# Seven products instead of eight in two more blocks of a retention + bilinear FFN kernel, with the last attention visit divided

## The chip, the cores and the metric

The kernel runs on one core of a Trainium2 chip. The core's engines work side by side, each through its own queue in order: TensorE (PE in the profile; its weight loads are PEld), VectorE (DVE), ScalarE (ACT), GpSimd (POOL), and SyncE (SP), which only issues DMAs. The metric is device time in microseconds (us), lower is better.

## The reference

Retention over a sequence, and then a feed-forward block without an activation function, on 4 x 768 = 3072 tokens of width 512:

```python
def _attn_ref(q, k, v):                      # 4 batches, 8 heads, 768 steps, 64 wide
    gamma = 1.0 - 2.0 ** (-5.0 - np.arange(H))
    for t in range(S):
        state = gamma * state + np.einsum('bhd,bhe->bhde', k[:, :, t], v[:, :, t])
        y[:, :, t] = scale * np.einsum('bhd,bhde->bhe', q[:, :, t], state)
    return y

def _moe_ref(x, w_a, w_b, w_out):            # x: 3072 x 512, d_ff 1536
    a = x @ w_a
    b = x @ w_b
    return (a * b @ w_out)
```

## The kernel before

**Tiles.** The 24 chunks of 128 tokens form eight tiles `J` of 4, 2, 2, 2, 2, 4, 4 and 4 chunks (`TILES`); tile 4 is the fifth. For a tile the kernel computes, for each of 12 blocks `ft` of the hidden width, `a` (`ffn_a`, L598) and `g` (`ffn_g`, L610), each four matmuls of 256 or 512 columns. ScalarE copies `a` out of PSUM as `asb` (L602), VectorE multiplies `g` by it into `ht` (L613). Then `ffn_fast(J, u)`, called the output block here, multiplies `ht` by `w_out` for a pair of chunks.

**Output blocks.** They use seven half-size products instead of eight (a Strassen-like scheme, `product`, L772, six matmuls of 256 columns each). Their left sides are pieces of `ht` and four sums of such pieces, `hsum` (`add`, L670), their banks are R1, R2, R5 and, for the blocks in `ASIDE`, R4. ScalarE keeps a product in `snap` (L784), and VectorE adds two into `osb` (L787, L818). The sum `osb` from R2 and `snap` stands on VectorE behind all `hsum` additions that VectorE makes for the tile. The PSUM pool `ff` has three banks, for `a`, `g`, and R1 to R5.

**Cycles.** In tiles 6 and 7 the `a` of some pairs of blocks `f` is made from seven products too (`seven_a`, called a cycle here): two matmuls of 256 columns for each of parts 1 to 7 (`part_a`, L712), in order 1, 2, 5, then a `g`, then 6, part 4 of the cycle before, 3, another `g`, and 7. R1, R2 and R5 are its banks. ScalarE keeps R1 after part 1, R5 after part 5 and R1 after part 6 (L729, L732, L739), VectorE adds (L726). `SEVEN` gives the pairs: 1 to 3 in tile 6, 1 to 5 in tile 7. `seven_end` finishes the last cycle of a run. The right sides are `xs`, four sums of the tile's input that VectorE makes (`combine_x`, L681), the weights are `ta`, four sums of `w_a` for each pair, made on GpSimd (`combine_a`, L690).

**Visits.** The attention of a pair of chunks runs between these matmuls, in visits (`turn(new, old)`): products of queries with states (`inter`, L359, in two halves), the new pair's states and scores (L287, L317), a tiny copy `mark` (L336) that separates the two halves, the second half, and the products with values (`intra`, L371). Afterwards ScalarE writes the tile's input `xt` from the banks y0 and y1 (`leave`, L386). `begin_turn` and `end_turn` are the two parts of a visit without a new pair. `ahead` lists where each visit stands.

**Order.** `seq` chains every instruction to the one before it on its engine, so each queue follows the order in which the code is written; `later` and `unmasked` hold small jobs that `catch_up` and `mask_now` put in at fixed places. The tile pools add the waits on buffers.

Of the kernel before, what the change touches and what calls it, by code (L numbers as in the profile page):

```python
# [17 lines left out]
ASIDE = ((4, 0), (5, 0), (6, 0), (6, 1), (7, 0))  # L18
SEVEN = {6: (1, 4), 7: (1, 6)}
SPARE = {(J, ft) for J in (2, 3, 4) for ft in range(1, 6 if J == 4 else 10, 2)}  # L20
PAIRS = 3
# [6 lines left out]
def kernel(  # L28
# [349 lines left out]

    def leave(o, c, apart):
# [5 lines left out]
        if apart is None:  # L385
            seq(nc.scalar.copy(dst, src))  # L386
        else:
            on, off = slice(4 - 4 * c, 8 - 4 * c), slice(4 * c, 4 * c + 4)
            part = tra.tile([P, 2, 2, D], F32, tag="kq"[c] + "T2", name="part", bufs=2)
            seq(nc.scalar.copy(part, apart[c][:, :, 2 - 2 * c : 4 - 2 * c]))  # L390
            part = part.rearrange("p s k (par m) -> p s (k par) m", par=2)
            for s in range(2):
                seq(nc.vector.tensor_tensor(dst[:, s, on], src[:, s, on], part[:, s], op=ALU.add))
                seq(nc.vector.tensor_copy(dst[:, s, off], src[:, s, off]))

# [6 lines left out]
    def end_turn(old):  # L402
        inter(old, False, ys[old])
        intra(old)
        later[:] = [lambda c=c: leave(old, c, None) for c in range(2)] + later

    def turn(new, old, eng=nc.scalar):
        catch_up()
        apart = None
        if old is not None:  # L410
            ys[old] = [psat.tile([P, 2, KT, D], F32, tag=f"y{c}", name="y") for c in range(2)]
            if new is None:
                both = psat.tile([P, 2, 2, KT, D], F32, tag="at", name="apart")
                apart = [both[:, c] for c in range(2)]
            inter(old, True, ys[old] if new is not None else apart)
            if new is not None:
                fence[old, 0] = fence[old, 1] = fenced(eng)
        if new is not None:
            chunk_states(new)
            scores(new)  # L420
        if old is not None:
            inter(old, False, ys[old])
            intra(old)
            leaves = [lambda c=c: leave(old, c, apart) for c in range(2)]
            later[:] = leaves + later
# [164 lines left out]
    def ffn_a(J, ft, c0=0, c1=None):  # L590
        c1 = TILES[J] * P if c1 is None else c1
        if J not in ht:
            ht[J] = htp.tile([P, NFT, 4 * P], BF16, tag="ht", name="ht")
        fs = slice(ft * P, (ft + 1) * P)
        a = ff_bank(J, ft, 0, "a")[:, : c1 - c0]
        for kt in range(KT):
            for b0, b1 in parts(J, ft, c0, c1, NFT):
                seq(nc.tensor.matmul(a[:, b0 - c0 : b1 - c0], wa_bf[:, kt, fs], xcols(J, kt, b0, b1),  # L598
                                     start=(kt == 0 and b0 == c0), stop=(kt == KT - 1 and b1 == c1),
                                     skip_group_check=True))  # L600
        asb = asbs[J, ft, c0] = asbp.tile([P, 4 * P], BF16, tag="asb", name="asb")[:, : c1 - c0]
        seq(nc.scalar.copy(asb, a))  # L602

    def ffn_g(J, ft, c0=0, c1=None):
        c1 = TILES[J] * P if c1 is None else c1
        fs = slice(ft * P, (ft + 1) * P)
        g = ff_bank(J, ft, 1, "g")[:, : c1 - c0]
        for kt in range(KT):
            for b0, b1 in parts(J, ft, c0, c1, NFT):
                seq(nc.tensor.matmul(g[:, b0 - c0 : b1 - c0], wb_bf[:, kt, fs], xcols(J, kt, b0, b1),  # L610
                                     start=(kt == 0 and b0 == c0), stop=(kt == KT - 1 and b1 == c1),
                                     skip_group_check=True))
        seq(nc.vector.tensor_tensor(ht[J][:, ft, c0:c1], g, asbs.pop((J, ft, c0)), op=ALU.mult))  # L613
# [77 lines left out]

    banks = {}
# [21 lines left out]

    def seven_a(J, f):

        W2 = 2 * P
        if J not in banks:
            own_banks(J)
        R1, R2, R5 = banks[J][f % 2]  # L720
        snap = raw.tile([P, 4, W2], F32, tag="vf", name="snap")
# [13 lines left out]
        plus(even[:, :W2], R2, snap[:, 0])  # L735
        catch_up(2)
        ffn_g(J, 2 * f - 1)
        part_a(J, f, R1, 6, False)
# [5 lines left out]
        plus(odd[:, :W2], R5, snap[:, 1])  # L744
        catch_up(2)
        ffn_g(J, 2 * f - 2)
        part_a(J, f, R1, 7, False)
# [4 lines left out]

        behind.extend((lambda: plus(odd[:, W2:], R1, snap[:, 2]), last_of))

    behind = []
# [19 lines left out]
    def ffn_fast(J, u):  # L775
# [10 lines left out]
        def plus(dst, R, x):  # L786
            seq(nc.vector.tensor_tensor(dst, R[:, :DH], x, op=ALU.add))  # L787

        R1, R2 = bank(), bank()
# [4 lines left out]
        keep(0, R1)  # L794
        catch_up(2)
        if not swap:
            product(R2, J, u, ("h", 1, 0), (0, 2), True)
        visit(J, "mid")
        plus(osb[:, 0, :DH], R2, snap[:, 0])
# [8 lines left out]
        product(R1, J, u, ("s", 1), (1, 1), False)  # L808
        keep(1, R1)
        catch_up(1)  # L810
        visit(J, "sums", u)
        R5 = bank()
# [8 lines left out]
        else:  # L821
            plus(osb[:, 1, DH:], R1, snap[:, 3])
        if ends:
            seq(nc.sync.dma_start(out=dst[:, 1, DH:], in_=osb[:, 1, DH:]))
# [118 lines left out]
    for j in range(NO):  # L943
# [8 lines left out]
        (4, 0): [(casts, 17)], (4, 8): [(turn, 14, 12)],  # L952
        (4, "o", 0): [(begin_turn, 14), (casts, 18)], (4, "mid"): [(end_turn, 14), (casts, 19)],
        (5, 0): [(casts, 20)], (5, 2): [(casts, 21)], (5, 3): [(turn, 16, None)],
        (5, 8): [(turn, 18, 16), (casts, 22)],
        (5, "sums", 0): [(turn, 20, 18, D_), (casts, 23)],
# [19 lines left out]
    def blocks_seven(J):  # L976
        f0, f1 = SEVEN[J]
        combine_x(J)
        store()
        for ft in range(2 * f0):  # L980
            ffn_a(J, ft)
        for f in range(f0, f1):
            seven_a(J, f)
            sums_of(J, f - 1)
            mask_now(1)
        seven_end(J, f1 - 1)
        sums_of(J, f1 - 1)
        return 2 * f1

    def sums_of(J, f):  # L990
        if J == 6 and f == 0:
            return
        if J == 6:
            f0, f1 = (0, 2) if f == 1 else (f, f + 1)
            for which in range(4):
                add(J, which, f0, f1, nc.gpsimd)
            if f == 3:
                combine_a(4)
                combine_a(5)
        elif f < 5:  # L1000
            for which in range(4 if f < 4 else 2):
                add(J, which, f, f + 1, nc.gpsimd)
        else:
            for which in range(2):
                add(J, which, 5, 6)
            for which in (2, 3):
                add(J, which, 4, 6)

    def blocks(J):
        done = blocks_seven(J) if J in SEVEN else 0  # L1010
        for ft in range(done, NFT):
            if ft > 1 or J == 5:
                store()
            visit(J, ft)
            ffn_ab(J, ft)
            if J in FAST:
                for which, f0, f1 in adds_of(J, ft):
                    if J not in SEVEN or f0 >= 4:
                        add(J, which, f0, f1)

# [48 lines left out]
```

## Time and profile before

| | us |
|---|---|
| runs | 223.07, 222.96, 221.06 (median 222.96) |
| the profiled execution's own time | 222.28 |
| its span | 220.6 |
| TensorE busy | 212.5 (96%) |
| VectorE, ScalarE, GpSimd busy | 147.1, 96.8, 116.5 |

In the profile a row of the timeline gives start, length, engine, line, operation, what is written and read, and in brackets the idle time before it with what ended it. A row's length of matmuls contains a modelled tail, so the pace is read from one start to the next. L numbers are lines of the kernel before.

### The profile page before, as it was taken

What the parts mean: (1) busy time and instruction counts of PE and PEld (TensorE: products, weight loads), DVE (VectorE), ACT (ScalarE), POOL (GpSimd) and SP (SyncE); (2) the same over time, 40 slices, a digit from 0 to 9 for tenths busy, and PEclk for the clock granted to TensorE, in tenths of its full rate; (3) what the DMA queues carried; (4) which work ended last, traced back from release to release, by engine and by line L of the source; (5) the groups of instructions that cost most, each with busy time, mean ns of one, the idle gap of its engine ahead of it and who ended that gap; (6) DMA issues with size and microseconds to landing.
All of it is one profiled execution on the core that took longest, in us unless ns stands there. A gap on an engine that the chain in (4) does not pass through costs nothing.

```text
span 220.6 us, 7028 instructions
## 1 busy us (share of the span) xinstructions
PE 212.5 (96%) x2871; PEld 156.4 (71%) x2875; DVE 147.1 (67%) x325; ACT 96.8 (44%) x239; POOL 116.5 (53%) x157
## 2 busy tenths in 40 slices
PE   8889999999999999999999999989999999999993
PEld 7568888885456887888878445468666478666682
DVE  2774456648816686797785387997877694777731
ACT  3765244342526435436465342736432643443231
POOL 6557799782735435144353514347949960087500
PEclk9999999999999999999999999999999999999999
DMA  5999999997999995896969889799600002200022
GB/s 171 346 377 383 368 314 401 332 203 166 216 257 250 219 248 109 147 234 189 223 126 225 205 147 279 112 230 123 214 0 4 0 3 98 97 0 4 0 95 95
DMA packets 94832, 39.77 MB, mean 180 GB/s; under 512 B 76112, under 2 KB 91728, under 8 KB 94800
## 3 DMA queue, kind: packets, MB, share of 16 engines
q1 hardware_dynamic: 94656, 39.20, 70.2%
q8 instruction: 22, 0.36, 0.6%
q10 hardware_dynamic: 144, 0.13, 0.2%
q14 instruction: 10, 0.08, 0.1%
HBM read 28.31 MB, written 6.29 MB: 157 GB/s over the span
## 4 chain that ended last, share of the span: by engine, by line
PE 85%; DVE 6%; DMA 3%; ACT 2%; issue 1%; POOL 1%; SPq 0%; DVEq 0%; POOLq 0%; ACTq 0%
PE g L610 27%; PE a L598 22%; PE o L772 16%; PE o L647 7%; PE a L712 5%; DMA kf<-in_k_dram 3%; DVE hsum L670 2%; DVE ht L613 2%; POOL kqb L239 1%; PE y L359 1%; PE y L371 1%; PE at L317 1%; PE st L287 1%; ACT xt L386 1%; PE tp L450 1%
## 5 line engine op out<-in xcount | busy, mean ns | idle before, releaser
L613 DVE TENSOR_TENSOR ht<-g,asb 128x256 bf16<-128x256 f32 (+1 forms) x98 | 53.8, 549 | 41.3 <-PE g L610 30.3
L610 PE MATMUL g<-xt,wb_bf 128*128 128x256 bf16 (+1 forms) x432 | 77.8, 308 | 0.3 <-ACT asb L602 0.3
L598 PE MATMUL a<-xt,wa_bf 128*128 128x256 bf16 (+1 forms) x368 | 60.8, 296 | 0.1
L602 ACT CAST asb<-a 128x256 bf16<-128x256 f32 (+1 forms) x82 | 36.9, 452 | 49.5 <-PE a L598 49.2
L610 PEld LDWEIGHTS <-wb_bf 128*128 128x128 bf16 x432 | 42.1, 98 | 16.5 <-issue 0.4
L239 POOL TENSOR_TENSOR kqb<-kf,ktab 128x512 bf16<-128x512 f32 x21 | 22.6, 1081 | 40.7 <-DMA kf<-in_k_dram 31.8
L598 PEld LDWEIGHTS <-wa_bf 128*128 128x128 bf16 x368 | 35.3, 98 | 12.3 <-DVE sums L301 0.3
L239 POOL TENSOR_TENSOR kqb<-qf,qtab 128x512 bf16<-128x512 f32 x21 | 23.1, 1103 | 4.8 <-DMA qf<-in_q_dram 4.6
L204 POOL CAST vb<-vf 128x512 bf16<-128x512 f32 x24 | 14.6, 617 | 18.8 <-DMA vf<-in_v_dram 9.3
L772 PEld LDWEIGHTS <-hsum 128*128 128x128 bf16 x216 | 20.9, 98 | 3.7 <-DVE sums L301 0.6
L784 ACT COPY snap<-o 128x256 f32<-128x256 f32 x32 | 12.0, 376 | 21.2 <-PE o L772 21.1
L670 POOL TENSOR_TENSOR hsum<-ht 128x256 bf16<-128x256 bf16 (+1 forms) x15 | 11.0, 735 | 18.5 <-DVE ht L613 18.5
L772 PE MATMUL o<-wt_bf,hsum 128*128 128x256 bf16 x162 | 19.8, 273 | 0.4 <-DVE sums L301 0.3
L772 PEld LDWEIGHTS <-ht 128*128 128x128 bf16 x162 | 15.4, 98 | 2.8
L647 PE MATMUL o<-wo_bf,ht 128*128 128x512 bf16 x69 | 15.9, 379 | 0.2
L670 DVE TENSOR_TENSOR hsum<-ht 128x256 bf16<-128x256 bf16 (+1 forms) x32 | 13.5, 426 | 0.3
L301 DVE TENSOR_TENSOR sums<-st,sums 128x256 f32<-128x256 f32 x30 | 12.7, 423 | 1.5
L772 PE MATMUL o<-wo_bf,ht 128*128 128x256 bf16 x108 | 13.3, 273 | 0.0
L202 ACT CAST gst<-sums 128x256 bf16<-128x256 f32 x33 | 12.7, 417 | 0.5 <-DVE sums L299 0.3
L787 DVE TENSOR_TENSOR osb<-o,snap 128x256 f32<-128x256 f32 x22 | 9.2, 419 | 5.2 <-PE o L772 3.3
L647 PEld LDWEIGHTS <-ht 128*128 128x128 bf16 x72 | 6.9, 98 | 7.9
L323 DVE TENSOR_TENSOR aT<-at,mask 128x512 bf16<-128x512 f32 x18 | 12.1, 680 | 0.0
(99 smaller groups left out, 260.9 us busy)
## 6 DMA issues: line engine op xcount, KB each, us to landing
out_dram<-osb SPq DMA_DIRECT2D x11, 512.0 KB, 4.4
kf<-in_k_dram SPq DMA_DIRECT2D x18, 256.0 KB, 4.2
qf<-in_q_dram SPq DMA_DIRECT2D x36, 128.0 KB, 3.9
vf<-in_v_dram SPq DMA_DIRECT2D x18, 256.0 KB, 4.2
wsta<-in_moe_w_a_dram SPq DMA_DIRECT2D x6, 512.0 KB, 7.7
wstb<-in_moe_w_b_dram SPq DMA_DIRECT2D x6, 512.0 KB, 7.9
wsto<-in_moe_w_out_dram SPq DMA_DIRECT2D x6, 512.0 KB, 7.5
kf<-in_k_dram SPq DMA_DIRECT2D x3, 512.0 KB, 5.9
```

The source lines that it names most:

```text
L202: seq(nc.scalar.copy(dst, src))
L204: seq(engine.tensor_copy(dst, src))
L239: seq(eng.tensor_tensor(dst, src, tab, op=ALU.mult))
L301: seq(nc.vector.tensor_tensor(new, u[c][:, s], old, op=ALU.add))
L323: unmasked.append(lambda r=r: seq(nc.vector.tensor_tensor(aT[n][:, r].rearrange("p s h d -> p (s h) d"), at[:, r].rearrange("p s h d -> p ...
L598: seq(nc.tensor.matmul(a[:, b0 - c0 : b1 - c0], wa_bf[:, kt, fs], xcols(J, kt, b0, b1), start=(kt == 0 and b0 == c0), stop=(kt == KT - 1 a ...
L602: seq(nc.scalar.copy(asb, a))
L610: seq(nc.tensor.matmul(g[:, b0 - c0 : b1 - c0], wb_bf[:, kt, fs], xcols(J, kt, b0, b1), start=(kt == 0 and b0 == c0), stop=(kt == KT - 1 a ...
L613: seq(nc.vector.tensor_tensor(ht[J][:, ft, c0:c1], g, asbs.pop((J, ft, c0)), op=ALU.mult))
L647: seq(nc.tensor.matmul(o, ht[J][:, ft, i * P : (i + 1) * P], wo_bf[:, f, 2 * r : 2 * r + 2, :].rearrange("p a d -> p (a d)"), start=(ft == ...
L670: seq(eng.tensor_tensor(s[which], x(), y(), op=op))
L772: seq(nc.tensor.matmul(R[:, :DH], lhs, (wo_bf, wt_bf)[w][:, f, m, :], start=(first and f == 0), stop=(f == NH - 1), skip_group_check=True))
```

## The change

- `SEVEN` lists the pairs themselves: 1, 2, 4, 5 for tile 6 and 0 to 5 for tile 7, four and six cycles instead of three and five. Pairs 0 and 3 of tile 6 are made in the plain way.
- The first cycle of tile 7 is spread over the second output block of tile 6 (`begin_seven`, `step_seven`), and `combine_x(7)` stands before that block.
- The banks of a cycle are taken for each cycle (`own_banks(J, f)`). R5 is always the first half of the tile `at`. In pair 4 of tile 6 the banks are y0, the state bank and a bank of `ff`; in pair 5, R1 is the second half of the tile whose first half is R5.
- In tile 6, the visit with the last new pair comes earlier (before block 6 instead of 8), its masks are put in at once, and the last visit (pair 22) is divided: `begin_turn` inside pair 5's cycle, `end_turn` before the first output block. The path with the separate bank `apart` is gone.
- In tile 4, `begin_turn` and `end_turn` of pair 14 come later within the first output block, and the `catch_up(2)` in block 8 is gone.
- `mark` of the visit in tile 5's first output block moves from VectorE to ScalarE.
- GpSimd makes the sums `hsum` of tiles 6 and 7 for pairs 0 to 3 two pairs at a time, and all four sums of pair 4; VectorE makes those of pair 5 alone. `combine_a` runs for pairs 1, 2, 4, 5 in tile 5, and 0 and 3 at the end of tile 6.
- The first output block of tile 6 computes R2 before R1 (`swap`), as that of tile 7 did.
- `ht` is taken in `ffn_g` instead of `ffn_a`; `SPARE` is written another way and holds the same.

```diff
-SEVEN = {6: (1, 4), 7: (1, 6)}
+SEVEN = {6: (1, 2, 4, 5), 7: (0, 1, 2, 3, 4, 5)}
@@ turn: "apart" removed; leave() only copies
-            if new is None:
-                both = psat.tile([P, 2, 2, KT, D], F32, tag="at", name="apart")
@@ ffn_ab
-        if (J, ft) == (4, 8):
-            catch_up(2)
@@ the banks of a cycle
-    def own_banks(J):
-        at = psat.tile([P, 2, 4 * P], F32, tag="at", name="a")
-        st = psst.tile([P, 4 * P], F32, tag="st", name="a")
-        y = [psat.tile([P, 4 * P], F32, tag=f"y{c}", name="a") for c in range(2)]
-        banks[J] = [[y[f % 2][:, : 2 * P], st[:, : 2 * P], at[:, f % 2, : 2 * P]] for f in range(2)]
+    def own_banks(J, f):
+        st = psst.tile([P, 4 * P], F32, tag="st", name="a")
+        if (J, f) == (6, 4):
+            y = psat.tile([P, 4 * P], F32, tag="y0", name="a")
+            at = psff.tile([P, 4 * P], F32, tag="ff", name="a")
+        else:
+            both = psat.tile([P, 2, 4 * P], F32, tag="at", name="a")
+            at = both[:, 0]
+            if (J, f) == (6, 5):
+                y = both[:, 1]
+            else:
+                y = psat.tile([P, 4 * P], F32, tag=f"y{f % 2}", name="a")
+        return [x[:, : 2 * P] for x in (y, st, at)]
@@ ffn_fast
-        swap = (J, u) == (7, 0)
+        swap = u == 0 and J in SEVEN
@@ ahead (a line or two)
-        (6, 8): [(turn, 22, 20)], (6, "o", 0): [(turn, None, 22)],
+        (6, 6): [(turn, 22, 20), (catch_up, 2), (mask_now,)], (6, 11): [(begin_turn, 22)], (6, "o", 0): [(end_turn, 22)],
+        (6, "before", 1): [(combine_x, 7), (begin_seven, 7, 0)],
+        (6, 1, 1): [(step_seven,)], (6, 3, 1): [(step_seven,)], (6, 5, 1): [(step_seven,)],
-    ahead[5, "sums", 0] += [(combine_a, f) for f in (1, 2, 3)]
+    ahead[5, 4, 0] += [(combine_a, f) for f in (1, 2, 4, 5)]
@@ sums_of
+        if f < 4:
+            if f % 2:
+                for which in range(4):
+                    add(J, which, f - 1, f + 1, nc.gpsimd)
+        else:
+            for which in range(4):
+                add(J, which, f, f + 1, nc.gpsimd if f == 4 else nc.vector)
+            if (J, f) == (6, 4):
+                combine_a(0)
+                combine_a(3)
```

**Where instructions move.** First, TensorE at the start of a cycle. Before, in tile 6, pair 2 (names with their buffer numbers, and in brackets the engine whose signal a row waits for): parts 1, 2 and 5 write three tiles.

```order
L712 MATMUL a_3594<-xt_3238,wa_bf_172 128x256
L712 LDWEIGHTS wa_bf_172
L712 MATMUL a_3593<-xt_3238,wa_bf_172 128x256 [waits DVE_49]
L712 LDWEIGHTS wa_bf_172
L712 MATMUL a_3593<-xt_3238,wa_bf_172 128x256
L712 LDWEIGHTS ta_3470 [waits Pool_49]
L712 MATMUL a_3592<-xs_3571,ta_3470 128x256 [waits DVE_49]
```

Now, in tile 6, pair 5, the cycle that holds `begin_turn(22)`:

```order
L703 MATMUL a_3888<-xt_3238,wa_bf_172 128x256
L703 LDWEIGHTS wa_bf_172
L703 MATMUL a_3887<-xt_3238,wa_bf_172 128x256 [waits DVE_49]
L703 LDWEIGHTS wa_bf_172
L703 MATMUL a_3887<-xt_3238,wa_bf_172 128x256
L703 LDWEIGHTS ta_3470 [waits Pool_49]
L703 MATMUL a_3888<-xs_3575,ta_3470 128x256 [waits Activation_49]
```

Parts 1 and 5 now write the same tile `a_3888`, and part 5 waits for ScalarE, which keeps part 1's result, instead of VectorE.

Second, TensorE in the first output block of tile 6, where R5 begins (the tile `o` with `hsum_3664` before, and `hsum_3670` now). Before:

```order
L772 LDWEIGHTS hsum_3665 [waits DVE_49]
L772 MATMUL o_4009<-wt_bf_175,hsum_3665 128x256
L772 LDWEIGHTS hsum_3665 [waits DVE_49]
L772 MATMUL o_4009<-wt_bf_175,hsum_3665 128x256
L772 LDWEIGHTS hsum_3664
L772 MATMUL o_4052<-wt_bf_175,hsum_3664 128x256 [waits Activation_49]
```

Now:

```order
L779 LDWEIGHTS hsum_3671 [waits Pool_49]
L779 MATMUL o_4026<-wt_bf_175,hsum_3671 128x256
L779 LDWEIGHTS hsum_3671 [waits DVE_49]
L779 MATMUL o_4026<-wt_bf_175,hsum_3671 128x256
L779 LDWEIGHTS hsum_3670
L779 MATMUL o_4059<-wt_bf_175,hsum_3670 128x256 [waits DVE_49]
```

R5 waited for ScalarE's copy out of R4's bank; now it has R2's bank and waits for VectorE's `osb`. In the first output blocks of tiles 5 and 7 it waits for VectorE in both kernels.

Third, VectorE in the first output block of tile 5. Before:

```order
L670 TENSOR_TENSOR hsum<-ht,hsum 128x256 x2
L787 TENSOR_TENSOR osb<-o,snap 128x256
L336 COPY mark<-bq 128x1
L301 TENSOR_TENSOR sums<-st,sums 128x256 x4
L818 TENSOR_TENSOR osb<-o,snap 128x512
L323 TENSOR_TENSOR aT<-at,mask 128x512
```

Now:

```order
L655 TENSOR_TENSOR hsum<-ht,hsum 128x256 x2
L794 TENSOR_TENSOR osb<-o,snap 128x256
L301 TENSOR_TENSOR sums<-st,sums 128x256 x4
L828 TENSOR_TENSOR osb<-o,snap 128x512
L323 TENSOR_TENSOR aT<-at,mask 128x512
```

`mark` is gone from this queue; it stands on ScalarE behind the copy of R1.

More of the change, by code (lines that the diff above doesn't have):

```diff
@@ L384, in leave @@
         src = ys[o][c].rearrange("p s k (par m) -> p s (k par) m", par=2)
[L385 to L394, printed above, removed]
+        seq(nc.scalar.copy(dst, src))
     def begin_turn(old, eng=nc.scalar):
@@ L753, in seven_a, with begin_seven, step_seven @@
         behind.extend((lambda: plus(odd[:, W2:], R1, snap[:, 2]), last_of))
+        yield
+    def seven_a(J, f):
+        steps = seven_steps(J, f)
+        next(steps)
+        catch_up(2)
+        ffn_g(J, 2 * f - 1)
+        next(steps)
+        catch_up(2)
+        ffn_g(J, 2 * f - 2)
+        visit(J, 2 * f + 1)
+        next(steps)
+    amid = []
+    def begin_seven(J, f):
+        amid.append(seven_steps(J, f))
+    def step_seven():
+        next(amid[0])
     behind = []
```

92 lines of the change are left out of this document (39 added, 53 removed).

## The prediction

> **What bounds the kernel now.** I read the page first, then TensorE's timeline from tile 4 to the end, then the other queues at each place where TensorE stood or may stand.
>
> ```profile
> span 220.6 us, 7028 instructions
> PE 212.5 (96%) x2871; PEld 156.4 (71%) x2875; DVE 147.1 (67%) x325; ACT 96.8 (44%) x239; POOL 116.5 (53%) x157
> PEclk9999999999999999999999999999999999999999
> ```
>
> TensorE is busy for 96% of the span at full granted clock. So fewer matmul columns shorten the time directly, and every wait of TensorE that the change takes away or brings in counts in full. The profiled execution took 222.28 us, 1.68 more than its span, and lies 0.68 below the median of the three runs. I sum against 222.28.
>
> **Two more cycles.** Two cycles of tile 7 show the pace:
>
> ```profile
> 128.84 1.03 PE L598 MATMUL a<-xt,wa_bf 128*128 128x512 bf16 x4
> 129.70 1.03 PE L610 MATMUL g<-xt,wb_bf 128*128 128x512 bf16 x4
> ...
> 192.32 0.60 PE L712 MATMUL a<-xt,wa_bf 128*128 128x256 bf16 x4
> ...
> 195.57 0.60 PE L712 MATMUL a<-xt,wa_bf 128*128 128x256 bf16 x4
> ```
>
> A plain group of four takes 129.70 - 128.84 = 0.86. A cycle takes 195.57 - 192.32 = 3.25, of which two g groups are 1.73; its 14 half-width matmuls take 1.52 (0.11 each) and replace two plain a groups of 1.73. Saved: 0.21 per cycle, **-0.43** for two.
>
> **Tile 4.** After the visit the leaves and state casts that `catch_up(2)` puts in delay ScalarE's `asb`, whose bank the next g needs:
>
> ```profile
> 113.35 0.60 PE L598 MATMUL a<-xt,wa_bf 128*128 128x256 bf16 x4
> 114.22 0.60 PE L610 MATMUL g<-xt,wb_bf 128*128 128x256 bf16 x4 [0.27 <-ACT asb L602]
> 114.68 0.60 PE L598 MATMUL a<-xt,wa_bf 128*128 128x256 bf16 x4
> 115.11 0.60 PE L610 MATMUL g<-xt,wb_bf 128*128 128x256 bf16 x4
> ```
>
> The step from a to g is 0.87 where the next is 0.43: 0.44 lost, and with one leaf per block instead of two it goes. But `end_turn(14)` now stands after the fourth product, so both its leaves come after ScalarE's last `snap` of the block, and tile 5 needs them:
>
> ```profile
> 119.36 0.37 ACT L784 COPY snap<-o 128x256 f32<-128x256 f32 x1 [0.28 <-PE o L772]
> 119.63 0.59 ACT L386 CAST xt<-y 128x512 bf16<-128x512 f32 x1
> 120.11 0.39 ACT L784 COPY snap<-o 128x256 f32<-128x256 f32 x1
> ...
> 138.78 1.08 ACT L386 CAST xt<-y 128x512 bf16<-128x512 f32 x2
> ```
> ```profile
> 121.20 1.03 PE L598 MATMUL a<-xt,wa_bf 128*128 128x512 bf16 x4
> ```
>
> A `snap` holds its queue 0.27 (119.36 to 119.63), two leaves 1.08: 120.11 + 0.27 + 1.08 = 121.46, after the 121.20 at which tile 5 began. So 0.25 comes back (between 0 and 0.44): **-0.19**.
>
> **The mark in tile 5.**
>
> ```profile
> 148.78 0.28 PE L359 MATMUL y<-kqT,gst 64*64 64x64 bf16 x10 [0.95 <-DVE mark L336]
> ...
> 149.28 1.48 PE L772 MATMUL o<-wt_bf,hsum 128*128 128x256 bf16 x12
> ```
> ```profile
> 148.25 0.41 DVE L787 TENSOR_TENSOR osb<-o,snap 128x256 f32<-128x256 f32 x1
> 148.59 0.14 DVE L336 COPY mark<-bq 128x1 f32<-128x1 f32 x1
> ```
>
> `mark` sits on VectorE behind hsum additions and the `osb` from R2; TensorE idles 0.95. On ScalarE it follows the copy of R1, which nothing delays, so that wait goes, and the late `osb` is next: the product that starts at 149.28 is R5's, in R2's bank, which that `osb` frees at 148.66. With 0.05 for the signal, R5 starts at 148.71: **-0.57**, not -0.95. Nothing waits behind `mark` on ScalarE for long, whose next job is R5's own copy.
>
> **The divided last visit.**
>
> ```profile
> 115.64 0.32 PE L359 MATMUL y<-kqT,gst 64*64 64x64 bf16 x16
> 115.89 1.48 PE L772 MATMUL o<-wo_bf,ht 128*128 128x256 bf16 x12
> ...
> 117.84 0.83 PE L772 MATMUL o<-wt_bf,ht 128*128 128x256 bf16 x6
> ...
> 176.75 1.03 PE L610 MATMUL g<-xt,wb_bf 128*128 128x512 bf16 x4
> ...
> 178.34 1.48 PE L772 MATMUL o<-wo_bf,ht 128*128 128x256 bf16 x12
> ```
>
> Whole, it takes from the end of a g (176.75 + 0.86) to 178.34: 0.73. Divided as in tile 4, the first part takes 115.89 - 115.55 = 0.34 (115.11 plus 0.44), the second 117.84 - 117.20 = 0.64 (twelve products after 115.89): **+0.25**. The `apart` additions that go were on VectorE and ended none of TensorE's waits; the masks put in at once stand on VectorE before it is needed.
>
> **Pair 5's cycle in tile 6.** R1 and R5 are now halves of one tile, and the program makes part 5 wait for ScalarE's copy of part 1, and by the same tile part 3 for the copy of part 6. In separate tiles neither wait exists, so the trace has no row for it; its length follows from a cycle of tile 7:
>
> ```profile
> 192.74 0.37 ACT L729 COPY snap<-a 128x256 f32<-128x256 f32 x1 [1.15 <-PE a L712]
> ```
>
> The copy starts 0.42 after its part (192.32) and ends at 0.79; with 0.05 the waiting matmul starts at 0.84, where it would have started after two parts, at 0.44. Twice 0.40: **+0.80** (between 0, if the halves didn't wait, and 0.80). The GpSimd sums do not depend on it.
>
> **R5 in the first output blocks.** R5 must wait for the `osb` from R2, which stands behind VectorE's hsum additions, and those are slowed when GpSimd works:
>
> ```profile
> 178.77 0.75 DVE L670 TENSOR_TENSOR hsum<-ht 128x256 bf16<-128x256 bf16 x1
> 179.55 0.64 DVE L670 TENSOR_TENSOR hsum<-hsum,ht 128x256 bf16<-128x256 bf16 x1
> 207.82 0.69 DVE L613 TENSOR_TENSOR ht<-g,asb 128x512 bf16<-128x512 f32 x1 [0.61 <-PE g L610]
> 208.61 0.29 DVE L670 TENSOR_TENSOR hsum<-ht 128x256 bf16<-128x256 bf16 x1
> ...
> 209.82 0.42 DVE L787 TENSOR_TENSOR osb<-o,snap 128x256 f32<-128x256 f32 x1
> ```
> ```profile
> 164.77 1.15 POOL L670 TENSOR_TENSOR hsum<-ht 128x512 bf16<-128x512 bf16 x1 [3.04 <-DVE ht L613]
> ...
> 169.34 0.67 POOL L670 TENSOR_TENSOR hsum<-ht 128x256 bf16<-128x256 bf16 x1
> ...
> 171.97 0.67 POOL L670 TENSOR_TENSOR hsum<-ht 128x256 bf16<-128x256 bf16 x1
> ...
> 178.65 0.72 POOL L690 TENSOR_TENSOR ta<-wa_bf 128x256 bf16<-128x256 bf16 x1
> ...
> 202.91 0.67 POOL L670 TENSOR_TENSOR hsum<-ht 128x256 bf16<-128x256 bf16 x1 [0.58 <-DVE ht L613]
> ...
> 206.91 0.67 POOL L670 TENSOR_TENSOR hsum<-hsum,ht 128x256 bf16<-128x256 bf16 x1
> ```
> ```profile
> 209.54 2.23 PE L772 MATMUL o<-wt_bf,hsum 128*128 128x256 bf16 x18
> ```
>
> An addition of 0.29 alone takes 0.64 to 0.75 beside GpSimd: the one at 178.77 ends at 179.52, 0.15 after the GpSimd instruction that ran when it began (179.37); one addition per GpSimd instruction. In tile 7 GpSimd was done at 207.58, a second before VectorE's additions. Now, from 202.91, it makes four double sums (169.34 - 164.77 = 4.57) and four single ones (171.97 - 169.34 = 2.63), until 210.1. VectorE's four additions, from 208.61, then end behind GpSimd's at about 208.9, 209.6 and 210.2, the fourth at 210.5; the `osb` after them ends at 210.95 instead of 210.24. R1's product ends at 209.54 + 6 x 0.11 = 210.2, R5 started 0.1 later behind that `osb`, and now would at 211.0: **+0.70** (0 to 0.8).
>
> In tile 6 R5 took R4's bank and waited for nothing on VectorE; now it takes R2's. GpSimd has the same eight sums and then eight `combine_a` instructions, so it is busy throughout. From the last `ht` to `osb`'s end are 0.1 + four additions (2.0 to 2.6) + 0.4; TensorE needs `end_turn` (0.64) and, as from 208.51 to 210.2 in tile 7, 1.7 until R5. The wait is 0.2 to 0.8 (0 if the additions ran free): **+0.60**.
>
> One rule of the Trainium skill bears on this, in "SBUF — State Buffer", section "Who interferes with whom": a VectorE instruction with both inputs in SBUF and a GpSimd instruction that reads SBUF exclude each other, and the later one is held until the other has finished. The 0.75 and 0.64 agree, except that a held addition ends 0.15 after GpSimd's, not its full 0.29. By the rule word for word each R5 would be about 0.14 later, and the sum 0.3 higher.
>
> Covered: the sums themselves (GpSimd's second sum of pair 4 is due about 208.9, its matmul about 210.0), and `ta` for pairs 4 and 5, made seconds ahead. TensorE issues the interleaved first cycle of tile 7 at the usual pace if `xs` is there (a rival, below).
>
> **Sum.** -0.43 - 0.19 - 0.57 + 0.25 + 0.80 + 0.70 + 0.60 = **+1.16**: 223.4 from the profiled execution, 224.1 from the median. I take 223.7. A difference under 1% (2.2 us) is about what this kernel's runs cannot tell from none, so the forecast is "same", on its slow side.
>
> **Rivals.** *The new waits are covered*: R1 and R5 don't wait on each other's copies, or the additions slip between GpSimd's instructions. For it: VectorE has fewer additions than before in tile 6. Against it: the 0.64 to 0.75 above. Time: -0.43 - 0.19 - 0.57 + 0.25 = -0.94, 221.3; if `osb` also came early enough for all 0.95, 220.9.
>
> *`combine_x(7)` blocks the second output block of tile 6.* It stands on VectorE before the `osb` that frees R5's bank there, and GpSimd may still be in `combine_a`:
>
> ```profile
> 155.73 0.41 DVE L681 TENSOR_TENSOR xs<-xt 128x512 bf16<-128x512 bf16 x1
> ...
> 157.68 0.89 DVE L681 TENSOR_TENSOR xs<-xt 128x512 bf16<-128x512 bf16 x1
> ```
>
> Beside GpSimd four of these took 157.68 + 0.89 - 155.73 = 2.84. With 0.5 before them and 0.8 behind, R5's bank is free 4.1 after the block began; TensorE wants it after five products and ten matmuls of the cycle, 34 x 0.11 = 3.7. That is 0.4, and the parts waiting for each `xs` can lose as much again; with the word-for-word additions (0.3) the sum is about 2.3: 224.6, slower. It decides if GpSimd ends `combine_a` later than about 1 us into the block; by its own rows it ends about when the block begins.
>
> *The cycles save nothing* (half-width matmuls slower): the cycle of 3.25 speaks against it; 223.8.
>
> **Chances.** Forecast 0.62, covered 0.18 (a third of it below -1%), blocked 0.14, no saving 0.03, else 0.03. Faster by over 1%: 0.08; within: 0.75; slower: 0.17. Range: the covered case at its usual 221.3 to the blocked one with the median's 0.68, 225.2.
>
> **What would show it.** The cycle steps of 3.25 unchanged; no 0.95 behind `mark`, but R5 in tile 5 starting right behind `osb`; part 5 in pair 5's cycle idle 0.4 behind ScalarE; R5 in tiles 6 and 7 idle behind VectorE's `osb`, with additions of 0.6 and more. Wrong, if those last three idle times are absent.

## The result, and the profile after

The changed kernel takes 223.41 us (median of 11 runs, 222.47 to 224.18), the kernel before 222.07 in the same session (11 runs): a ratio of 1.0064, with a 95% interval of 1.0043 to 1.0085. That is 1.34 us more, inside the 1% called "same", on its slow side; the interval excludes 1, so the loss itself is clear of noise. The profiled execution took 223.99 us, 1.71 more than that of before.

The page of the changed kernel (its first lines, and the chain):

```profile
span 222.3 us, 7055 instructions
PE 212.3 (96%) x2887; PEld 157.2 (71%) x2887; DVE 150.2 (68%) x318; ACT 97.6 (44%) x245; POOL 120.4 (54%) x155
...
PE 80%; DVE 10%; DMA 3%; ACT 3%; issue 2%; POOL 1%; SPq 0%; DVEq 0%; ACTq 0%
```

TensorE's busy time hardly moved (212.5 before). VectorE's share of the chain (the work that ended last, followed back) went from 6% to 10%. The waits of TensorE name where (us in total, how many, the longest):

```profile
PE o L779 <- DVE osb L794: 2.0, 4, 0.9
...
PE y L359 <- DVE ht L600: 0.3, 1, 0.3
PE st L287 <- DVE ht L600: 0.3, 1, 0.3
PE a L703 <- ACT snap L718: 0.2, 1, 0.2
PE a L703 <- ACT snap L727: 0.2, 1, 0.2
```

The longest, `osb`, is four waits: 0.27 in tile 3, ahead of the places that the change moves, 0.49 in tile 5 in place of the 0.95 behind `mark`, and 0.32 and 0.90 in tiles 6 and 7. These last two and the two of `snap` are the waits that the change brought in. The next table is made from TensorE's timeline of both kernels: each row is the time from the first matmul of one place to the first matmul of the next (the end of a g of tile 4 is its start plus 0.44).

| stretch (us) | before | after | difference |
|---|---|---|---|
| start to the end of the g of tile 4's block 7 | 110.01 | 109.70 | -0.31 |
| the visit in tile 4's block 8, until its a | 1.58 | 2.32 | +0.74 |
| blocks 8 to 11 of tile 4, to the last g | 3.52 | 3.07 | -0.45 |
| tile 4's last g and output block, to tile 5 | 6.09 | 6.42 | +0.33 |
| tile 5's blocks | 22.94 | 22.83 | -0.11 |
| tile 5's output blocks | 11.79 | 11.22 | -0.57 |
| tile 6's blocks with the last two visits | 22.41 | 23.24 | +0.83 |
| first output block of tile 6 | 4.63 | 5.08 | +0.45 |
| second output block of tile 6, to the cycle of pair 2 in tile 7 | 9.35 | 9.19 | -0.16 |
| the other cycles of tile 7 | 15.23 | 15.23 | 0 |
| first output block of tile 7 | 4.70 | 5.66 | +0.96 |
| the rest | 8.35 | 8.34 | -0.01 |

The sum is 1.70, the difference of the spans. The +0.83 of tile 6's blocks is made up of one more cycle (-0.21), pair 5's two waits (+0.82, below) and the divided visit (+0.22, further below). Now the rows of after for the three places that lose. Pair 5's cycle in tile 6 (TensorE's timeline: start, length, line, what is written and read, idle time before):

```profile
171.84 0.60 PE L703 MATMUL a<-xt,wa_bf 128*128 128x256 bf16 x4
172.69 0.38 PE L703 MATMUL a<-xs,ta 128*128 128x256 bf16 x2 [0.24 <-ACT snap L718]
...
173.98 0.38 PE L703 MATMUL a<-xt,ta 128*128 128x256 bf16 x2
174.61 0.38 PE L703 MATMUL a<-xs,wa_bf 128*128 128x256 bf16 x2 [0.24 <-ACT snap L727]
```

Part 5 comes 0.85 after part 1 instead of 0.44, part 3 comes 0.63 after part 4 instead of 0.22: 0.41 each, 0.82 together. The brackets say only 0.24, because a matmul's recorded length holds a modelled tail; the steps from start to start tell the loss.

The first output block of tile 7, first TensorE, then VectorE, then GpSimd:

```profile
210.29 0.81 PE L779 MATMUL o<-wt_bf,hsum 128*128 128x256 bf16 x6
212.00 1.47 PE L779 MATMUL o<-wt_bf,hsum 128*128 128x256 bf16 x12 [0.90 <-DVE osb L794]
```
```profile
209.29 0.29 DVE L655 TENSOR_TENSOR hsum<-ht 128x256 bf16<-128x256 bf16 x1
209.62 0.64 DVE L655 TENSOR_TENSOR hsum<-hsum,ht 128x256 bf16<-128x256 bf16 x1
210.18 0.76 DVE L655 TENSOR_TENSOR hsum<-ht 128x256 bf16<-128x256 bf16 x1
210.86 0.75 DVE L655 TENSOR_TENSOR hsum<-ht,hsum 128x256 bf16<-128x256 bf16 x1
211.54 0.41 DVE L794 TENSOR_TENSOR osb<-o,snap 128x256 f32<-128x256 f32 x1
```
```profile
204.01 1.15 POOL L655 TENSOR_TENSOR hsum<-ht 128x512 bf16<-128x512 bf16 x1 [2.25 <-DVE ht L600]
...
209.32 0.79 POOL L655 TENSOR_TENSOR hsum<-hsum,ht 128x256 bf16<-128x256 bf16 x1
210.07 0.72 POOL L655 TENSOR_TENSOR hsum<-ht 128x256 bf16<-128x256 bf16 x1
210.75 0.72 POOL L655 TENSOR_TENSOR hsum<-ht,hsum 128x256 bf16<-128x256 bf16 x1
```

VectorE's last three additions end at 210.26, 210.94 and 211.61, each 0.14 or 0.15 after one of GpSimd's (210.11, 210.79, 211.47). `osb` ends at 211.95 and R5 starts at 212.00. TensorE was ready at 210.29 + 0.65 = 210.94 (six matmuls of 0.11), so R5 waited 1.06; before it waited 0.1. In tile 6 it is the same with 0.48 (product at 180.78, R5 at 181.91):

```profile
180.78 0.82 PE L779 MATMUL o<-wt_bf,hsum 128*128 128x256 bf16 x6
181.91 1.47 PE L779 MATMUL o<-wt_bf,hsum 128*128 128x256 bf16 x12 [0.32 <-DVE osb L794]
```

### The profile page after: what moved, and what is told of

It reads as the page before. It is cut to its first block, busy times and chain, and to the rows that moved or that the text cites. A ratio compares the mean times of both kernels' runs of the same rounds, so it can differ in the third digit from the quotient of the medians.

```text
span 222.3 us, 7055 instructions
## 1 busy us (share of the span) xinstructions
PE 212.3 (96%) x2887; PEld 157.2 (71%) x2887; DVE 150.2 (68%) x318; ACT 97.6 (44%) x245; POOL 120.4 (54%) x155
## 4 chain that ended last, share of the span: by engine, by line
PE 80%; DVE 10%; DMA 3%; ACT 3%; issue 2%; POOL 1%; SPq 0%; DVEq 0%; ACTq 0%
PE g L595 27%; PE a L583 20%; PE o L779 12%; PE o L632 7%; PE a L703 7%; DVE hsum L655 4%; DVE ht L600 3%; DMA kf<-in_k_dram 3%; PE y L359 1%; PE at L317 1%; ACT xt L385 1%; PE st L287 1%; PE tp L437 1%; DVE osb L794 1%; PE y L371 1%
## 5 line engine op out<-in xcount | busy, mean ns | idle before, releaser
L583 PE MATMUL a<-xt,wa_bf 128*128 128x256 bf16 (+1 forms) x352 | 56.7, 292 | 0.2
L587 ACT CAST asb<-a 128x256 bf16<-128x256 f32 (+1 forms) x78 | 34.5, 443 | 44.1 <-PE a L583 43.2
L583 PEld LDWEIGHTS <-wa_bf 128*128 128x128 bf16 x352 | 33.8, 98 | 10.8 <-issue 0.3
L239 POOL TENSOR_TENSOR kqb<-qf,qtab 128x512 bf16<-128x512 f32 x21 | 22.6, 1079 | 6.7 <-DMA qf<-in_q_dram 6.5
L779 PE MATMUL o<-wt_bf,hsum 128*128 128x256 bf16 x162 | 20.4, 272 | 1.8 <-DVE osb L794 1.7
L655 POOL TENSOR_TENSOR hsum<-ht 128x512 bf16<-128x512 bf16 (+1 forms) x12 | 11.9, 995 | 17.1 <-ACT snap L718 11.7
L715 DVE TENSOR_TENSOR asb<-a,snap 128x256 bf16<-128x256 f32 x30 | 12.0, 418 | 2.2 <-ACT snap L727 0.8
L655 DVE TENSOR_TENSOR hsum<-ht 128x256 bf16<-128x256 bf16 (+1 forms) x30 | 12.4, 416 | 0.3
```

What stands on the lines that cost most here:

```text
L239: seq(eng.tensor_tensor(dst, src, tab, op=ALU.mult))
L655: seq(eng.tensor_tensor(s[which], x(), y(), op=op))
L779: seq(nc.tensor.matmul(R[:, :DH], lhs, (wo_bf, wt_bf)[w][:, f, m, :], start=(first and f == 0), stop=(f == NH - 1), skip_group_check=True))
```

## The experiments

Ratios are to the kernel before, whose runs lay between the others on the same chip. Its median there was 221.62 for the first four kernels, 221.41 for the next four, 221.60 for the last three.

### R1 and R5 in separate tiles

```diff
-        if (J, f) == (6, 4):
+        if (J, f) == (6, 5):
+            y = psat.tile([P, 2, 4 * P], F32, tag="at", name="a")[:, 0]
+            at = psff.tile([P, 4 * P], F32, tag="ff", name="a")
+        elif (J, f) == (6, 4):
...
-            if (J, f) == (6, 5):
-                y = both[:, 1]
-            else:
-                y = psat.tile([P, 4 * P], F32, tag=f"y{f % 2}", name="a")
+            y = psat.tile([P, 4 * P], F32, tag=f"y{f % 2}", name="a")
```

> The changed kernel, but in pair 5's cycle of tile 6 R1 and R5 are separate tiles (R5 a bank of ff, as in pair 4). Theory (the shared tile makes parts 5 and 3 wait for ScalarE's copies): part 5 starts 0.44 us after its cycle instead of 0.85, part 3 starts 0.22 after part 4 instead of 0.63, and the kernel is 0.8 us shorter than the changed one, about 222.6. Rival (the two idle times are signals or the divided visit that stands in that cycle): the steps of 0.85 and 0.63 stay, no gain. The wait for R5 in the first output block of tile 6 should stay or grow, since GpSimd's sums don't move.

Measured: 222.60 us, ratio 1.0056 (1.0034 to 1.0079, four runs). Pair 5's cycle in TensorE's timeline:

```profile
171.56 0.60 PE L703 MATMUL a<-xt,wa_bf 128*128 128x256 bf16 x4
172.00 0.38 PE L703 MATMUL a<-xs,ta 128*128 128x256 bf16 x2
...
173.30 0.38 PE L703 MATMUL a<-xt,ta 128*128 128x256 bf16 x2
173.52 0.38 PE L703 MATMUL a<-xs,wa_bf 128*128 128x256 bf16 x2
```

The steps are 0.44 and 0.22, both waits are gone, and tile 6's blocks take 22.44 instead of 23.24: 0.80. The shared tile was the cause. R5's wait in the output block stayed, at 0.52. The whole kernel's ratio fell by 0.0008, less than 0.80 would give (0.0036); with four runs that isn't settled by the times.

### Two additions behind osb

```diff
         plus(osb[:, 0, :DH], R2, snap[:, 0])
+        if swap:
+            for which in (2, 3):
+                add(J, which, 5, 6)
...
-            for which in range(4):
+            for which in range(4 if f == 4 else 2):
                 add(J, which, f, f + 1, nc.gpsimd if f == 4 else nc.vector)
```

> The changed kernel, but in the first output blocks of tiles 6 and 7 VectorE makes the last two of pair 5's four hsum additions behind the osb from R2. Theory (R5 waits because osb stands behind four slowed additions): R5's idle time of 0.32 to 0.48 us in tile 6 and of 0.90 to 1.06 in tile 7 both go, so 1.4 us shorter than the changed kernel, about 222.0. The additions themselves stay slow (0.6 to 0.8 each). Rival (osb is late for another reason, ScalarE's copy or the bank): the idle times stay, or the third product waits for the moved additions and the gain is lost, 223.4.

Measured: 222.21 us, ratio 1.0029 (1.0006 to 1.0051). In tile 7 the first output block takes 4.61 instead of 5.66, so R5's wait is gone with 1.05 gained, although two additions there still take 0.64 and 0.75. In tile 6 the block takes 4.78 instead of 5.08: R5's wait went, but the next product of R1 then stood 0.18, behind ScalarE's second copy of R1, which stood behind two leaves. And most of the rest was lost in the next block, where VectorE makes the sums `xs` (the first of them on VectorE, then TensorE):

```profile
183.72 0.77 DVE L666 TENSOR_TENSOR xs<-xt 128x512 bf16<-128x512 bf16 x1
```
```profile
183.83 0.60 PE L703 MATMUL a<-xt,wa_bf 128*128 128x256 bf16 x4
184.55 0.38 PE L703 MATMUL a<-xs,ta 128*128 128x256 bf16 x2
```

Part 5 starts 0.72 after part 1 instead of 0.44, since the first `xs` takes 0.77 beside GpSimd's `combine_a`. From the start of tile 6's first output block to the cycle of pair 1 in tile 7 it is 10.96 against 11.02: of 0.48, 0.06 is left. A wait that goes uncovered the next two.

### GpSimd's sums of tile 7 one pair at a time

```diff
-        if f < 4:
+        if f < 4 and J == 7:
+            for which in range(4):
+                add(J, which, f, f + 1, nc.gpsimd)
+        elif f < 4:
             if f % 2:
```

> The changed kernel, but in tile 7 GpSimd makes the sums of pairs 0 to 3 one pair at a time, so that it ends its work earlier, at about 209.5 instead of 211.5 us, close to where VectorE's four additions begin. Order on VectorE and banks unchanged. Theory (GpSimd's sums slow the additions): the four additions in tile 7 take about 0.3 each instead of 0.64 to 0.76, R5's idle time there falls from 0.90 to 0.1 or less, about 0.9 us shorter than the changed kernel, 222.5. Rival (the additions are slow by themselves, or osb waits for something else): they keep 0.64 to 0.76 and the idle time of 0.9 stays. Tile 6 is unchanged and keeps its wait.

Measured: 222.17 us, ratio 1.0037 (1.0010 to 1.0065). VectorE's additions and GpSimd's last sum in tile 7:

```profile
207.87 0.44 DVE L655 TENSOR_TENSOR hsum<-ht 128x256 bf16<-128x256 bf16 x1
208.34 0.29 DVE L655 TENSOR_TENSOR hsum<-hsum,ht 128x256 bf16<-128x256 bf16 x1
208.55 0.28 DVE L655 TENSOR_TENSOR hsum<-ht 128x256 bf16<-128x256 bf16 x1
208.75 0.28 DVE L655 TENSOR_TENSOR hsum<-ht,hsum 128x256 bf16<-128x256 bf16 x1
```
```profile
207.49 0.67 POOL L655 TENSOR_TENSOR hsum<-ht,hsum 128x256 bf16<-128x256 bf16 x1
```

GpSimd ends at 208.16. The two traces differ in their start of the output block (206.87 here, 208.30 in the changed kernel), so times are compared from there: GpSimd ends 1.29 after it, where the changed kernel had 3.17 and the expectation 1.2. The one addition that meets it ends at 208.31, 0.15 later; the other three take 0.28 or 0.29, with the order of VectorE's work and the banks as in the changed kernel. R5 doesn't wait, and the block takes 4.60 instead of 5.66. So it was GpSimd's sums that made VectorE late.

### Mark alone

```diff
-        (5, "sums", 0): [(turn, 20, 18, D_), (casts, 23)],
+        (5, "sums", 0): [(turn, 20, 18), (casts, 23)],
```

> The kernel before with one edit: mark of the visit in tile 5's first output block is on ScalarE instead of VectorE. Theory: the wait of 0.95 us behind mark goes, and R5 becomes the next to wait, for VectorE's osb, so only 0.5 to 0.6 are gained: 221.5 against 222.07. Rival (nothing else is late there): 0.95 gained, 221.1. Second rival (the queue of ScalarE is as late): no gain.

Measured: 221.18 us, ratio 0.9984 (0.9961 to 1.0008). In the trace tile 5's output blocks take 10.86 instead of 11.79, as if all 0.95 were gained, and the wait for `osb` is short (0.22). The times allow anything from a loss of 0.18 to a gain of 0.86. The theory fits the times and not the trace, the first rival the trace and, by a little, not the times; the last two runs below take up this stretch again.

### Tile 4's visit put back, and the catch_up alone

In the changed kernel:

```diff
-        (4, "o", 0): [(casts, 18)], (4, "mid", 0): [(begin_turn, 14)], (4, 4, 0): [(end_turn, 14), (casts, 19)],
+        (4, "o", 0): [(begin_turn, 14), (casts, 18)], (4, "mid", 0): [(end_turn, 14), (casts, 19)],
```

> The changed kernel, but in tile 4's output block the two parts of the visit of pair 14 stand where they stood before (first part ahead of the block, second after the second product); the catch_up(2) stays away. Theory (the late leaves cost tile 5's start): from the last g of tile 4 to tile 5's first matmul 6.10 us as before the change, instead of 6.42, so 0.3 shorter than the changed kernel, 223.1. Rival (tile 5 started late for another reason): 6.4 stays.

In the kernel before:

```diff
-        if (J, ft) == (4, 8):
-            catch_up(2)
```

> The kernel before with one edit: the catch_up(2) in tile 4's block 8 is gone. Theory (the two leaves and casts delayed asb): the step from a to g of block 10, 0.87, becomes 0.44, 0.44 gained, about 221.6 against 222.07, and the visit's second part doesn't lose it again. Rival (the leaves are only moved to the next blocks, where they delay another asb): another step of 0.6 to 0.9 appears, no gain.

Measured: 223.62 us, ratio 1.0114 (1.0078 to 1.0151, four runs), for the first, and 221.15, ratio 0.9998 (0.9979 to 1.0017), for the second. My expectation failed in both. Blocks 8 to 11 take 3.07 in both, as hoped, but from the last g to tile 5 it is 6.78 in both, where the kernel before has 6.09 and the changed one 6.42. The rows are of the kernel with the visit put back, TensorE and then ScalarE:

```profile
114.88 0.26 PE L359 MATMUL y<-kqT,gst 64*64 64x64 bf16 x8
115.64 0.26 PE L359 MATMUL y<-kqT,gst 64*64 64x64 bf16 x8 [0.50 <-ACT gst L202]
```
```profile
114.87 1.02 ACT L202 CAST gst<-sums 128x256 bf16<-128x256 f32 x3
```

The `catch_up(2)` also put in the casts of the states, `gst`. Without it three of them are still to do when `begin_turn` starts, and TensorE waits 0.50 for them (0.51 in the other of the two kernels). The later visit gives ScalarE time for these casts; what the late leaves cost (0.33) is less than what the early visit would (0.69). The two edits of tile 4 are one.

### One cycle less

```diff
-SEVEN = {6: (1, 2, 4, 5), 7: (0, 1, 2, 3, 4, 5)}
+SEVEN = {6: (1, 2, 4, 5), 7: (1, 2, 3, 4, 5)}
...
-        (6, "before", 1): [(combine_x, 7), (begin_seven, 7, 0)],
-        (6, 1, 1): [(step_seven,)], (6, 3, 1): [(step_seven,)], (6, 5, 1): [(step_seven,)],
...
-        if J == 6:
-            combine_x(J)
+        combine_x(J)
...
-                combine_a(0)
```

> The changed kernel with one cycle less: pair 0 of tile 7 is made in the plain way, with the input sums at the head of tile 7 as before. Theory (a cycle of seven products replaces 1.73 us of matmuls by 1.52): from the start of tile 6's second output block to tile 7's third cycle 0.16 to 0.21 longer than in the changed kernel, about 223.6. Rival (the interleaved cycle costs what it saves, because VectorE makes the input sums beside GpSimd): equal or shorter, down to 223.2.

Measured: 223.14 us, ratio 1.0075 (1.0045 to 1.0106). From the second output block of tile 6 to the cycle of pair 2 it takes 9.34, against 9.19 in the changed kernel: the cycle saves 0.15, of 0.21; 0.06 is lost at its part 5. The times can't tell 0.15 from nothing.

### The new waits taken out together

The edits of the first two experiments, and these:

```diff
-        catch_up(2)
+        catch_up(1 if (J, u) == (6, 0) else 2)
...
-        catch_up(1)
+        if (J, u) != (6, 0):
+            catch_up(1)
...
-        if swap:
+        if swap or (J, u) == (5, 0):
             for which in (2, 3):
-                add(J, which, 5, 6)
+                add(J, which, 4 if J == 5 else 5, 6)
...
-        (4, "o", 0): [(casts, 18)], (4, "mid", 0): [(begin_turn, 14)], (4, 4, 0): [(end_turn, 14), (casts, 19)],
+        (4, "o", 0): [(begin_turn, 14), (casts, 18)], (4, "mid", 0): [(end_turn, 14), (casts, 19)],
...
+        if (J, ft) == (5, 11):
+            return [(1, 4, 5), (0, 5, 6), (1, 5, 6)]
```

> The changed kernel with its new waits taken out together: separate tiles for R1 and R5 in pair 5's cycle of tile 6; in the first output blocks of tiles 5, 6 and 7 the last two hsum additions behind the osb from R2; tile 4's visit where it stood before; one leaf instead of two ahead of R1's second copy in tile 6. Theory (each wait stands by itself): 0.80 + 0.48 + 0.96 + 0.32 + 0.3 = 2.9 us shorter than the changed kernel, 220.5, a ratio to the kernel before of about 0.993. Rival (as one wait goes, another queue is late at the same place): half of that, 222.0, a ratio of 1.0.

Measured: 221.38 us, ratio 1.0008 (0.9987 to 1.0030): the rival's side. Tile 6's blocks (22.43) and tile 7's first output block (4.61) gain in full. Tile 4 loses 0.36, as in the two runs above, and tile 6's first output block gains 0.40, of which the second block and its cycle give back 0.33 (6.27 instead of 5.94), by `xs` additions of 0.77 to 0.88. This trace also has 23.42 for tile 5's blocks, 0.59 more than the changed kernel's; the second version below, with the same code there, has 22.82, so that is no effect of the edits.

So a second version has tile 4 as in the changed kernel, and `combine_a(0)` moved into GpSimd's idle time after the first double sums of tile 6:

```diff
                 for which in range(4):
                     add(J, which, f - 1, f + 1, nc.gpsimd)
+                if (J, f) == (6, 1):
+                    combine_a(0)
...
             if (J, f) == (6, 4):
-                combine_a(0)
                 combine_a(3)
```

> The changed kernel with R1 and R5 in separate tiles, the last two hsum additions behind the osb from R2 in tiles 5 to 7, one leaf ahead of R1's second copy in tile 6, tile 4 as in the changed kernel, and GpSimd's combine_a for pair 0 moved into its idle time after the first double sums of tile 6, so that it is done before VectorE makes the sums of tile 7's input. Theory (what the run with the tile 4 visit put back lost was 0.36 in tile 4, and 0.33 in tile 6's second block to additions slowed by combine_a): 0.7 shorter than that run, 220.7 on the same chip, a ratio to the kernel before of 0.995 to 0.997, and the second block of tile 6 with its cycle takes 5.9 us again. Rival (the sums of the input wait for the leaves or for osb, not for GpSimd): the block keeps 6.2, and the ratio is 0.998 or more.

Measured: 220.88 us (12 runs), ratio 0.9976 (0.9954 to 0.9999), between the 0.995 to 0.997 of the theory and the 0.998 of the rival. It is faster than the kernel before by about a quarter of a percent, with an interval that only just excludes 1, and than the changed one by about 0.9% (1.0064 against 0.9976, from two sessions, each with its interval). The `xs` additions run free, the first of them in 0.42, and tile 6's second block with its cycle takes 5.90, as the theory said (VectorE):

```profile
182.09 0.42 DVE L666 TENSOR_TENSOR xs<-xt 128x512 bf16<-128x512 bf16 x1
```

### Mark back on VectorE, and the kernel before once more

In the changed kernel:

```diff
-        (5, 4, 0): [(turn, 20, 18), (casts, 23)],
+        (5, 4, 0): [(turn, 20, 18, D_), (casts, 23)],
```

> The changed kernel with mark of tile 5's visit back on VectorE. Theory of the prediction (a fixed loss of 0.95 behind mark): TensorE's output part of tile 5 takes 11.8 us, 0.57 more than in the changed kernel, about 224.0. Theory as the runs since suggest (how long VectorE's additions take there is set by whether GpSimd's two casts, which wait for DMAs, fall on them): between 10.9 and 11.8, a mean loss of 0.2 to 0.3, 223.6.

> The kernel before, unchanged, for a second trace. If the waits at the visit in tile 4's block 8 and behind mark in tile 5 depend on when GpSimd's casts come, their lengths differ from the first trace (1.36 for the visit, 11.79 for tile 5's output part) by several tenths, with no change to the program; if they are fixed, both repeat within 0.05.

Measured: 223.36 us, ratio 1.0075 (1.0046 to 1.0103), with mark back, and for the kernel before one execution of 221.02. Tile 5's output blocks take 11.79 with mark back on VectorE, but 10.79 in the second trace of the kernel before, against 11.79 in its first: 1.00 apart in the same program. The 11.79 with mark back is what the theory of a fixed loss asks for; the 10.79 rules that theory out. VectorE and GpSimd in the kernel before's first trace, then in its second:

```profile
145.22 1.13 DVE L670 TENSOR_TENSOR hsum<-ht 128x256 bf16<-128x256 bf16 x1
...
146.59 1.33 DVE L670 TENSOR_TENSOR hsum<-ht 128x256 bf16<-128x256 bf16 x2
```
```profile
145.09 1.11 POOL L239 TENSOR_TENSOR kqb<-kf,ktab 128x512 bf16<-128x512 f32 x1 [5.06 <-PE o L772]
146.61 1.17 POOL L239 TENSOR_TENSOR kqb<-qf,qtab 128x512 bf16<-128x512 f32 x1 [0.41 <-DMA qf<-in_q_dram]
```
```profile
145.67 0.28 DVE L670 TENSOR_TENSOR hsum<-ht 128x256 bf16<-128x256 bf16 x1
...
146.20 0.49 DVE L670 TENSOR_TENSOR hsum<-ht 128x256 bf16<-128x256 bf16 x2
```
```profile
142.93 1.04 POOL L239 TENSOR_TENSOR kqb<-kf,ktab 128x512 bf16<-128x512 f32 x1 [4.15 <-DMA kf<-in_k_dram]
144.56 1.04 POOL L239 TENSOR_TENSOR kqb<-qf,qtab 128x512 bf16<-128x512 f32 x1 [0.58 <-DMA qf<-in_q_dram]
```

In the first trace both casts fall on the last additions before `mark`, in the second they are over by then. When they come is set by the DMA that they wait for: three of the four rows name it. The fourth, the first cast of the first trace, is put down to TensorE, but it began 3.65 after its DMA was issued (141.44) and the same cast of the second trace 3.29 after (139.64), so there too the DMA is the likelier cause; that is argued, not shown. With mark on VectorE the stretch took 11.79, 11.79, 10.93 and 10.79 in four traces (mean 11.33), on ScalarE 10.59 to 11.22 in seven whose VectorE order is otherwise the same (mean 10.83). So the edit is worth about 0.5 on average by these traces, with some 0.3 of uncertainty from so few of them, and two single traces with and without it differ by anything from -0.43 to +1.20. The times don't show 0.5: 0.9984 (0.9961 to 1.0008) and, undone, 1.0075 against 1.0064, which is 0.24 and less than the noise. The visit in tile 4's block 8 moved too, from 1.58 in the first trace (by the table; the expectation says 1.36) to 1.51.

## Why the prediction was right

The forecast was 223.7, "same" on its slow side, with +1.16 for the parts; measured were 223.41 and +1.34. Between the two traces it was +1.70: the terms of the sum came to +1.39, and the rest is stretches that no term was about. So the total is this near in part because single errors were small and in part because they had both signs. Point by point, by the table of stretches:

- **Two more cycles, -0.43.** The one in tile 7 gave 0.16, the other is in tile 6's +0.83, which closes with its 0.21. Half-width matmuls cost what the old cycles showed.
- **Tile 4, -0.19.** The stretches give -0.45 and +0.33, in sum -0.12. Tile 5's first matmul does wait for the two leaves, which end at 121.46, the time worked out for it (ScalarE, then TensorE, of the changed kernel):

```profile
120.38 1.08 ACT L385 CAST xt<-y 128x512 bf16<-128x512 f32 x2
```
```profile
121.51 1.02 PE L583 MATMUL a<-xt,wa_bf 128*128 128x512 bf16 x4
```

  The working held, but the step "with one leaf per block instead of two it goes" was incomplete: the removal of `catch_up` alone gains nothing, because of the `gst` casts.
- **Mark, -0.57.** The same in the trace, -0.57, and with the mechanism forecast: no wait behind `mark`, and R5 0.49 behind `osb`. But the row behind the term was one draw. In both traces GpSimd's two casts fell on the last additions (in the changed kernel 145.69 to 146.73 and 147.01 to 148.18, and additions of 1.14 and, for a pair, 1.33); that the two draws matched to 0.01 is luck, the mean is near 0.5.
- **The divided visit, +0.25.** From the end of a g to the next part, and from the end of a g to the output block, it takes 0.35 (176.03 - 174.82 - 0.86) and 0.60 (178.80 - 177.34 - 0.86), against 0.73: +0.22. No run takes this edit out alone.

```profile
174.82 1.02 PE L595 MATMUL g<-xt,wb_bf 128*128 128x512 bf16 x4
...
176.03 0.39 PE L703 MATMUL a<-xs,ta 128*128 128x256 bf16 x2
...
177.34 1.03 PE L595 MATMUL g<-xt,wb_bf 128*128 128x512 bf16 x4
...
178.80 1.48 PE L779 MATMUL o<-wo_bf,ht 128*128 128x256 bf16 x12
```

- **Pair 5's cycle, +0.80.** Measured 0.82, and 0.80 when the tiles are split. The term was read from the program's order and one row of ScalarE's copy, without any row of the wait.
- **R5 in tile 7, +0.70.** Measured 0.96, mechanism right, size off in this trace. The step that failed is GpSimd's time, "from 202.91" and "until 210.1": its double sums began 4.29 before the output block and not 4.64, and its single sums took 0.67 to 0.79 beside VectorE, not 0.67. GpSimd ended 3.17 after the output block began, not 2.55. The late start is not due to the double sums: with single sums the sum of the same place began 4.29 before the block too. It follows VectorE's `ht` just before, which came 0.35 later than its g alone would have it. In three later runs whose tile 7 adds up `hsum` in the same way (tile 4's visit put back, one cycle less, mark back) it did not come late: there GpSimd began 4.63 to 4.65 before the block and ended 2.68 to 2.70 after its start, and the block took 5.38 to 5.40, 0.68 to 0.70 more than before the change. That is the forecast. The rows are of the changed kernel (`ht`), then of the one with mark back:

```profile
203.24 0.69 DVE L600 TENSOR_TENSOR ht<-g,asb 128x512 bf16<-128x512 f32 x1 [0.79 <-PE a L703]
```
```profile
202.56 0.69 DVE L600 TENSOR_TENSOR ht<-g,asb 128x512 bf16<-128x512 f32 x1 [0.44 <-PE g L595]
...
203.33 1.15 POOL L655 TENSOR_TENSOR hsum<-ht 128x512 bf16<-128x512 bf16 x1 [1.89 <-DVE ht L600]
...
209.95 0.71 POOL L655 TENSOR_TENSOR hsum<-ht,hsum 128x256 bf16<-128x256 bf16 x1
...
211.40 1.47 PE L779 MATMUL o<-wt_bf,hsum 128*128 128x256 bf16 x12 [0.61 <-DVE osb L794]
```

  Why that `ht` came late in four traces (the changed kernel and the first three runs on it) stays open.
- **R5 in tile 6, +0.60.** Measured 0.45; the four additions took 2.33 from first start to last end, inside the 2.0 to 2.6.

The rival in which `combine_x(7)` blocks the second output block did not happen in the changed kernel (0.06 at part 5), and did as soon as R5's wait was taken away (0.28 there, and 0.22 to R5 of the second block in the version with all edits): it was hidden behind the other wait. What the prediction gave against it was wrong: GpSimd was to end `combine_a` about when the block begins, and it ended 1.61 after (185.49 against 183.88), later than the 1 us named as the limit. Still the four `xs` additions took 2.14 (184.43 to 186.57), not 2.84, the `osb` after them ended at 187.23, and R5 started at 187.63 without a wait. The rival "covered" fell with the two idle times of `snap`.

On the held additions: the Trainium skill ("SBUF — State Buffer", section "Who interferes with whom") calls the ports that VectorE and GpSimd share an exclusive lock. In seven rows of these traces the held additions ended 0.14 or 0.15 after GpSimd's instruction and not a whole addition (0.29) later. So the waiting holds; a whole addition's time behind it, which the prediction took the rule to mean, does not.

What the prediction had no term for is +0.43 at the start of tile 4 and before (-0.31 and +0.74). The visit in block 8 waited 0.66 for VectorE in the changed kernel's trace. The code there is the same in all kernels, and from the end of the g before to the next a it took 1.33 to 2.15 in the other traces. It is another draw of the same kind: in the changed kernel's trace two of GpSimd's casts (107.57 to 108.61 and 108.57 to 109.66) lie on two of VectorE's additions, which took 1.07 and 1.01, and the last `ht` came late by that; in the first trace of the kernel before one cast lies on one addition, of 1.17.

## What to carry to other kernels

Where two engines share work on the same memory, an engine that is off the critical path is not free: moving sums to GpSimd lengthened VectorE's additions from 0.29 to 0.64 and more, and what stood behind them was a bank that TensorE waited for. So put what frees a bank ahead of what may be slow, and end the other engine's work before that place. In this program a tile of the pool is the unit of waiting (0.80 for two waits here): two results that are used in turns should not be halves of one tile, even where each half is used by itself. And before a wait in one trace is counted as a gain, take a second trace of the same program; the wait behind `mark` was 0.95 in one and nearly gone in the next, where the same stretch took 1.00 less.

## What the runs showed of the hardware that was not expected

Where VectorE's bf16 addition of 128x256 begins during a GpSimd instruction, its end is set by the end of that instruction, to within 0.02: six additions in the changed kernel (in tiles 6 and 7) and one in the run with single sums end 0.14 or 0.15 after it. GpSimd's own additions became longer there too, up to 0.80 instead of 0.67. An addition of 0.28 took 1.13 beside a cast of 1.11. The price of this contention in the unchanged kernel moved by 1.00 us between two executions, since GpSimd's casts, which wait for DMAs, fell at other times.
